# Three moves in a hand-written instruction order: copies of x ahead of squares, x ahead of a product, a crossbar transfer ahead of a load

## The chip, the cores and the metric

The kernel runs on one core of a Trainium2 chip. The core has five engines that run their own instruction streams: TensorE (PE in the profile, with its weight loads listed apart as PEld), VectorE (DVE), ScalarE (ACT), GpSimd (POOL) and SyncE (SP), and 16 DMA engines beside them. The metric is device time in microseconds (us). The kernel before the change takes 170.55 us, the median of three runs (170.48 to 170.65).

## The reference

The first part is a linear-attention recurrence over four batches, eight heads, 768 steps and 48 columns a head; the second is a two-layer network with a squared relu on its result:

```python
def _attn_ref(r, k, v, w, u):
    ...
    for t in range(S):
        kt, vt, rt = (k[:, :, t].copy(), v[:, :, t].copy(), r[:, :, t].copy())
        cur = np.einsum('bhd,bhe->bhde', u[None] * kt, vt)
        y[:, :, t] = np.einsum('bhd,bhde->bhe', rt, state + cur)
        state = w[None, :, :, None] * state + np.einsum('bhd,bhe->bhde', kt, vt)
    return y.astype(np.float32)

def _moe_ref(x, w_in, w_out):
    h = np.maximum(x @ w_in, 0.0)
    return (h * h @ w_out).astype(np.float32)
```

`x` is the result of the first part with the heads side by side: 3072 tokens of 384 values. `w_in` is 384 by 2048, `w_out` is 2048 by 384. Inputs and result are float32; the kernel multiplies in bfloat16.

## The kernel before

**Units and groups.** The 3072 tokens are cut into 24 units of 128 steps, each one chunk of one batch (`UNITS`). The recurrence is done chunk by chunk: inside a unit with matrices, between the units of a batch through a state S. Units are gathered in 14 groups for the network: 0, 1, 12 and 13 hold one unit each, the others two (group 2 is units 2 and 3, group 4 is units 6 and 7, group 8 is units 14 and 15).

**Steps.** Each piece of work is a step, named in a table, with its engine behind the colon (P, D, A, G, S for PE, DVE, ACT, POOL, SP) and the numbers of the buffers that it takes behind the slash. For a unit i the steps are, in order:

- `ld.r`, `ld.k`, `ld.v`: loads on SP's queue (line 322);
- `kh`, `rh`: k and r times powers of w, to bf16 (338, 341); `vb`: v to bf16;
- `P0`: r times k (344); `P1`: that times u (348); `du`: its sum over a head (351); `dv`: v times that sum (356);
- `T` and `Tc`: eight transposes of kh and rh on PE and one copy of them out of PSUM; later units use `XB` in their place, a transposing DMA (405);
- `A`: k against r (412); `Bm`: the masked copy of it (420); `Y`: the unit's output in PSUM (460, 462);
- `xs`: Y plus dv, to bf16 (493; for units 0 to 3 a plain copy); `U`, `ts`, `S`: the state's update (482, 499, 502);
- `X`: three transposes of xs on PE (507), and `xTc`: the copy of them to the network's input (line 252 on ACT, 254 on DVE); for units 12, 15 and 16 to 23 `xX` in their place, a transposing DMA (514) on SP's queue.

For a group g and a slice s of the hidden layer, `F1.g.s` multiplies x by a part of `w_in` into a PSUM bank (523), `re` is the relu out of the bank (533 on ACT, 535 on DVE), `sq` the square (540, 542). `F2.i.q` multiplies a quarter of the squares of unit i by `w_out` (551); four of them fill a bank that `os` copies and `out` writes to memory.

**What sets the order.** Nothing is scheduled: the string `ORDER` is read step by step, and each engine gets its steps in that order and runs them in that order. The loop behind it is

```python
    for step in ORDER.split():
        what, how = step.split(":")
        ...
        getattr(Do, name)(E[eng], *at)
```

The waits are put in when the program is built: an instruction waits for the last writer and the last readers of what it touches, through one counter for each engine. DMAs of SP and ACT use eight counters in turn, and each DMA also waits until the transfer that used its counter before it has landed, so that a place in SP's queue also decides which earlier transfer is waited for. Eight PSUM banks serve everything that PE writes; the bank numbers are those in the table. A step that wants a bank waits until the step that read the bank last is done: `F1.4.7`, for example, takes the bank that `ts.7` reads, `F1.4.5` the one that `ts.8` reads, and `F1.2.1` the one that `Tc.4` reads.

Of the kernel before, what the change touches and what calls it, by code (L numbers as in the profile page):

```python
# [31 lines left out]
Bp.1.0.1:D/4 UP.1:P/4/6 Bp.1.0.0:D/6 X.0:P/5 xs.1:A/1 xTc.0:D/0 S0.2:D Ap.1.1:P/2/0 X.1:P/3 F1.0.3:P/7 ts.3:D/0  # L32
xTc.1:A/1 F1.1.3:P/5 P0.3:G/3 P1.3:G du.2:D/2 re.0.3:D/0 F1.0.0:P/6 Bp.1.1.1:D/5 dv.2:G Wt.2:A re.0.0:A/1 W.1:G
du.3:D/3 ld.v.5:S/5 Wk.2:A F1.1.0:P/4 F1.1.1:P/3 dv.3:G re.1.0:A/2 F1.0.1:P/0 rh.5:G/4 re.1.3:A/3 Bp.1.1.0:D/7
YD.1:P/1/7 YI.3:P sq.1.3:A/0 re.0.1:A/4 W.2:G xs.3:D/2 xs.2:A/3 kh.4:D/5 re.1.1:A/5 sq.1.0:D/1 ld.k.6:S/6 W.3:G
F1.0.2:P/6 X.2:P/4 rh.4:D/5 sq.0.0:A/2 X.3:P/2 F1.1.2:P/5 W.0:G re.0.2:D/3 xTc.3:A/0 sq.0.3:A/3 xTc.2:D/0 re.1.2:A/2
P0.4:D/4 T.4:P/0 Tc.4:D/4 F1.2.4:P/1 F1.2.7:P/4 sq.1.2:D/4 F1.2.5:P/5 re.2.4:D/1 re.2.7:A/0 ld.r.6:S/6 sq.0.2:A/5
F1.2.1:P/0 re.2.5:D/2 re.2.1:A/3 sq.2.5:D/6 sq.0.1:D/7 F1.2.0:P/6 kh.5:D/4 F1.2.2:P/4 sq.2.1:A/8 F1.2.6:P/5 re.2.2:A/2
re.2.0:D/4 T.5:P/0 re.2.6:D/3 F2.0.2:P/4 F1.2.3:P/6 ld.r.7:S/7 Tc.5:A/5 P1.4:D du.4:D/4 sq.1.1:D/9 A.4:P/5/0 A.5:P/1/2
sq.2.6:A/10 re.2.3:A/5 sq.2.3:A/11 F2.0.1:P/4 sq.2.0:A/12 F2.0.3:P/4 vb.4:G/4 Bm.4.1:D/0 Bm.4.0:D/1 sq.2.7:A/13  # L40
# [615 lines left out]
```

## Time and profile before

| | us |
|---|---|
| median of three runs | 170.55 (170.48 to 170.65) |
| the profiled execution | 170.8 |
| its span, first to last instruction | 169.1 |
| PE matmuls busy | 161.0 |
| DVE busy | 137.4 |
| POOL busy | 101.3 |
| ACT busy | 100.6 |

The span is the part of an execution that the trace shows; 1.7 us of this one lie around it. The granted TensorE clock was 1.0 throughout. Matmuls are pipelined, so the busy time of PE counts the overlap of each with the next; where PE waits is read from the distance between starts. In rows of a timeline the first number is the start in us from the span's start, the second the length in us from the first start to the last end of the row's `xN` instructions, and a bracket gives the idle time of the engine before them with what the profile takes for its end.

### The profile page before, as it was taken

The numbers are of one execution on the slowest core, as the hardware profiler recorded it, in microseconds if no ns is written. First come the engines' busy times: TensorE is split into PE (matmuls) and PEld (weight loads), VectorE is DVE, ScalarE is ACT, GpSimd is POOL, SyncE is SP. The second block draws the span as 40 slices with busy tenths as digits, with TensorE's granted clock in tenths as the row PEclk, the third lists the DMA queues.
The fourth block names the chain that finished last, engine by engine and source line by source line (L and its number), as shares of the span: only waits on it lengthen the run. The fifth ranks groups of instructions, "written<-read, shape, count | busy, mean of one in ns | idle before, by whom it ended". The sixth has DMA issues, their size and how long they took to land.

```text
span 169.1 us, 4580 instructions
## 1 busy us (share of the span) xinstructions
PE 161.0 (95%) x1814; PEld 122.5 (72%) x1814; DVE 137.4 (81%) x253; ACT 100.6 (60%) x189; POOL 101.3 (60%) x125
## 2 busy tenths in 40 slices
PE   4998989999997999999999999999999999999993
PEld 1686878668765776888766878766888676898762
DVE  5699769987899999989998998998779975955400
ACT  4696596851771878349782467952099393254731
POOL 6799861295399318996699988399627760300000
DMA  5999999994999899899986999995939751330032
GB/s 135 323 237 192 217 212 203 180 211 88 194 211 170 177 190 222 194 199 188 227 123 134 223 174 214 219 186 144 179 70 202 204 134 25 103 88 0 6 140 93
DMA packets 97785, 28.02 MB, mean 166 GB/s; under 512 B 92530, under 2 KB 97524, under 8 KB 97764
## 3 DMA queue, kind: packets, MB, share of 16 engines
q1 hardware_dynamic: 93872, 22.42, 67.7%
q0 software_dynamic: 3008, 4.13, 12.4%
q10 hardware_dynamic: 884, 1.18, 2.3%
q8 instruction: 14, 0.23, 0.6%
q14 instruction: 7, 0.06, 0.1%
HBM read 20.45 MB, written 4.72 MB: 149 GB/s over the span
## 4 chain that ended last, share of the span: by engine, by line
PE 82%; DVE 8%; DMA 3%; issue 2%; SPq 2%; ACT 1%; DVEq 0%
PE bank L523 36%; PE bank L551 34%; PE bank L412 3%; DMA ldk<-in_k_dram 3%; PE bank L462 2%; SPq L326 2%; PE bank L460 2%; DVE Bm L393 2%; PE bank L482 2%; PE bank L565 2%; PE bank L507 1%; DVE Bm L420 1%; DVE du L351 1%; DVE P L348 1%; DVE P L344 1%
## 5 line engine op out<-in xcount | busy, mean ns | idle before, releaser
L523 PE MATMUL bank<-xT,W 128*128 128x256 bf16 (+1 forms) x672 | 70.2, 257 | 1.3 <-DVE xT L254 0.6
L551 PE MATMUL bank<-W,hq 128*128 128x384 bf16 x368 | 68.6, 326 | 0.0
L523 PEld LDWEIGHTS <-W 128*128 128x128 bf16 x672 | 56.8, 98 | 9.7 <-DVE xT L254 1.2
L533 ACT ACTIVATE hr<-bank 128x512 bf16<-128x512 f32 x67 | 38.9, 595 | 38.2 <-PE bank L523 29.8
L551 PEld LDWEIGHTS <-hq 128*128 128x128 bf16 x368 | 33.8, 97 | 18.5
L540 ACT ACTIVATE hq<-hr 128x512 bf16<-128x512 bf16 x70 | 41.0, 626 | 4.7 <-DVE hr L535 4.1
L420 DVE TENSOR_TENSOR Bm<-bank,maskJT 128x512 bf16<-128x512 f32 x40 | 25.6, 682 | 2.7 <-PE bank L412 2.7
L535 DVE TENSOR_SCALAR hr<-bank 128x512 bf16<-128x512 f32 x29 | 19.8, 686 | 6.7 <-PE bank L523 4.3
L348 POOL TENSOR_TENSOR P<-P,ub 128x384 f32<-128x384 f32 x15 | 16.0, 1070 | 13.2 <-DVE P L344 12.8
L356 POOL TENSOR_TENSOR dv<-ldv,du 128x384 f32<-128x384 f32 (+1 forms) x18 | 15.5, 872 | 13.4 <-DVE du L351 8.3
L341 POOL TENSOR_TENSOR rk<-ldr,Wt 128x384 bf16<-128x384 f32 x15 | 16.4, 1101 | 0.1
L542 DVE TENSOR_TENSOR hq<-hr 128x512 bf16<-128x512 bf16 x26 | 13.0, 513 | 2.0 <-ACT hr L533 1.8
L344 POOL TENSOR_TENSOR P<-ldr,ldk 128x384 f32<-128x384 f32 x13 | 13.3, 1021 | 1.5 <-DMA ldk<-in_k_dram 1.2
L502 POOL TENSOR_TENSOR S0W<-ts,WLm 128x384 bf16<-128x384 f32 x10 | 10.9, 1091 | 4.2 <-DVE ts L499 3.4
L338 POOL TENSOR_TENSOR rk<-ldk,Wk 128x384 bf16<-128x384 f32 x12 | 12.3, 1033 | 1.4 <-DMA ldk<-in_k_dram 1.4
L351 DVE TENSOR_REDUCE du<-P 128x8 f32<-128x384 f32 x24 | 12.9, 542 | 0.0
L493 DVE TENSOR_TENSOR xs<-bank,dv 128x384 bf16<-128x384 f32 x20 | 11.0, 551 | 2.3 <-POOL dv L356 0.7
L254 DVE COPY os<-bank 128x384 f32<-128x384 f32 x11 | 6.1, 551 | 6.5 <-PE bank L551 6.4
L252 ACT COPY xT<-bank 128x384 bf16<-128x384 bf16 x8 | 3.7, 480 | 10.8 <-PE bank L507 10.8
L499 DVE TENSOR_TENSOR ts<-bank,S0W 128x384 f32<-128x384 f32 x16 | 8.8, 549 | 1.1 <-POOL S0W L502 0.8
L462 PE MATMUL bank<-vb,Bm 128*128 128x48 bf16 x160 | 9.5, 184 | 0.0
L252 ACT COPY os<-bank 128x384 f32<-128x384 f32 (+2 forms) x14 | 6.3, 459 | 4.5 <-PE bank L551 2.5
(81 smaller groups left out, 175.0 us busy)
## 6 DMA issues: line engine op xcount, KB each, us to landing
ldr<-in_r_dram SPq DMA_DIRECT2D x20, 192.0 KB, 3.5
ldk<-in_k_dram SPq DMA_DIRECT2D x20, 192.0 KB, 4.0
ldv<-in_v_dram SPq DMA_DIRECT2D x20, 192.0 KB, 3.6
out_dram<-os SPq DMA_DIRECT2D x9, 192.0 KB, 2.3
W<-in_moe_w_in_dram POOLq DMA_DIRECT2D x4, 384.0 KB, 9.7
W<-in_moe_w_out_dram POOLq DMA_DIRECT2D x4, 384.0 KB, 7.4
out_dram<-os ACTq DMA_DIRECT2D x5, 192.0 KB, 3.9
out_dram<-os POOLq DMA_DIRECT2D x5, 192.0 KB, 3.7
```

The source lines that it names most:

```text
L341: e.tensor_mul(rk[slot[f"rk{i}"]][:, 0, :, 0:D], loaded("r", i), Do.factor("t", i % 2 if i < PAIRED else 2))
L344: e.tensor_mul(P0b[slot[f"P{i}"]], loaded("r", i), loaded("k", i))
L348: e.tensor_mul(t, t, bank("bu")[:, 0 : H * D].rearrange("p (h d) -> p h d", h=H) if i in EARLY_U else ub)
L351: e.tensor_reduce(dub[slot[f"dv{i}"]], P0b[slot[f"P{i}"]], axis=mybir.AxisListType.X, op=ALU.add)
L356: e.tensor_mul(dv_of(i) if i < PAIRED else dvb[slot[f"dv{i}"]], loaded("v", i), t)
L420: e.tensor_mul(Bmb[slot[f"Bm{i}{h}"]], heads(bank(f"bA{i}{h}"), 128), mask_b)
L523: e.matmul(hp[:, fi, :], W1[f // 4][:, c, 256 * (f // 2 % 2) : 256 * (f // 2 % 2 + 1)].rearrange("p (m j) -> p j m", j=2)[:, f % 2, :], xt ...
L533: e.activation(hr, hp, AF.Relu)
L535: e.tensor_scalar_max(hr, hp, 0.0)
L540: e.activation(hq, hr, AF.Square)
L542: e.tensor_mul(hq, hr, hr)
L551: e.matmul(bank(f"bO{i}")[:, 0:d_model], hqb[slot[f"hq{g},{f // m}"]][:, at : at + L], W2[q][:, f % 4, :], start=(seen[i] == 1 and f % 4 = ...
```

## The change

Only the table's order changes; no step, engine, buffer or bank does. Three places are touched.

1. **The copies of x of units 2 and 3** (around 23 to 25 us). `X.3` follows `X.2` as before, and `xTc.3` (ACT) and `xTc.2` (DVE) now come straight behind them. On ACT `xTc.3` goes ahead of the square `sq.0.0`; on DVE `xTc.2` goes ahead of `sq.1.0`, `rh.4` and `re.0.2`. On PE the first product that needs both, `F1.2.4`, goes ahead of the transposes `T.4`.
2. **x of units 6 and 7** (around 53 us). On DVE `xs.6` and `xs.7` go ahead of `P0.8`, the product of r and k of unit 8.
3. **The crossbar transfer of unit 15** (around 96 us). On SP `xX.15` goes ahead of the load `ld.v.16`. With it the two exchange counters: `xX.15` now waits for the landing of `ld.v.14`, and `ld.v.16` for that of `xX.12`; `out.8` still waits for `xX.15`, and `XB.19` for `ld.v.16`.

Of the table's lines one pair shows the form, that of the third place:

```diff
-Bm.14.0:D/4 Y.15:P/5 vb.14:G/7 du.14:D/0 F1.7.3:P/1 ld.v.16:S/1 kh.19:G/0 xs.15:D/4 xX.15:S/0 F1.7.2:P/7 re.7.3:A/0
+Bm.14.0:D/4 Y.15:P/5 vb.14:G/7 du.14:D/0 F1.7.3:P/1 kh.19:G/0 xs.15:D/4 xX.15:S/0 ld.v.16:S/1 F1.7.2:P/7 re.7.3:A/0
```

What it does to the engines' streams follows, with the buffers' numbers in the names. On DVE at the first place, `rk` on line 338 is `kh.4`, `xT2` is `xTc.2`, `hq_1` is `sq.1.0`, `rk` on line 341 is `rh.4`, `hr_3` is `re.0.2`, `P_4` is `P0.4` and `rkT` is `Tc.4`:

```order
 L254 CAST xs_2_122<-bank_7_181 128x384
 L338 TENSOR_TENSOR rk_5_80<-ldk_2_69,Wk_200 128x8x48
+L254 COPY xT2_0_127<-bank_4_178 128x3x128
 L542 TENSOR_TENSOR hq_1_137<-hr_2_132 128x512
 L341 TENSOR_TENSOR rk_5_80<-ldr_2_65,Wt_201 128x8x48
 L535 TENSOR_SCALAR hr_3_133<-bank_6_180 128x512
-L254 COPY xT2_0_127<-bank_4_178 128x3x128
 L344 TENSOR_TENSOR P_4_86<-ldr_2_65,ldk_2_69 128x384
 L254 COPY rkT_4_109<-bank_0_174 128x1024
```

The copy moved up three instructions; `P0.4` and `Tc.4` behind it have the same instructions ahead of them as before. On DVE at the second place, `hr_1` is `re.3.5`, `P_3` is `P1.9`, `P_4` is `P0.8`, `xs_1` and `xs_2` are `xs.6` and `xs.7`, `rk_3` is `kh.11` and `ts_0` is `ts.7`:

```order
 L535 TENSOR_SCALAR hr_1_131<-bank_4_178 128x512
 L348 TENSOR_TENSOR P_3_85<-P_3_85,ub_194 128x384
-L344 TENSOR_TENSOR P_4_86<-ldr_0_63,ldk_0_67 128x384
 L493 TENSOR_TENSOR xs_1_121<-bank_5_179,dv_2_94 128x384
 L493 TENSOR_TENSOR xs_2_122<-bank_4_178,dv_1_93 128x384
+L344 TENSOR_TENSOR P_4_86<-ldr_0_63,ldk_0_67 128x384
 L338 TENSOR_TENSOR rk_3_78<-ldk_1_68,Wk_200 128x8x48
 L499 TENSOR_TENSOR ts_0_172<-bank_5_179,S0W_3_193 128x384
```

`P0.8` moved behind the two sums; `kh.11` and `ts.7` stay behind all three. On SP at the third place, the loads of r are `ld.r.19` and `ld.r.18`, the transfer is `xX.15`, the load of v is `ld.v.16`, and the two writes are `out.9` and `out.6`:

```order
 L322 DMA ldr_1_64<-in_r_dram 128x8x48 x2
 L322 DMA ldr_2_65<-in_r_dram 128x8x48
+L514 DMA_TRANSPOSE xT2_0_127<-xs_4_124 128x3x128
 L322 DMA ldv_0_71<-in_v_dram 128x8x48
-L514 DMA_TRANSPOSE xT2_0_127<-xs_4_124 128x3x128
 L604 DMA out_0_dram<-os_1_165 128x384
 L604 DMA out_0_dram<-os_7_171 128x384
```

The transfer and the load changed places; the queue behind them is the same. POOL's stream does not change.

More of the change, by code (lines that the diff above doesn't have):

```diff
@@ L34 @@
 du.3:D/3 ld.v.5:S/5 Wk.2:A F1.1.0:P/4 F1.1.1:P/3 dv.3:G re.1.0:A/2 F1.0.1:P/0 rh.5:G/4 re.1.3:A/3 Bp.1.1.0:D/7
-YD.1:P/1/7 YI.3:P sq.1.3:A/0 re.0.1:A/4 W.2:G xs.3:D/2 xs.2:A/3 kh.4:D/5 re.1.1:A/5 sq.1.0:D/1 ld.k.6:S/6 W.3:G
-F1.0.2:P/6 X.2:P/4 rh.4:D/5 sq.0.0:A/2 X.3:P/2 F1.1.2:P/5 W.0:G re.0.2:D/3 xTc.3:A/0 sq.0.3:A/3 xTc.2:D/0 re.1.2:A/2
-P0.4:D/4 T.4:P/0 Tc.4:D/4 F1.2.4:P/1 F1.2.7:P/4 sq.1.2:D/4 F1.2.5:P/5 re.2.4:D/1 re.2.7:A/0 ld.r.6:S/6 sq.0.2:A/5
+YD.1:P/1/7 YI.3:P sq.1.3:A/0 re.0.1:A/4 W.2:G xs.3:D/2 xs.2:A/3 kh.4:D/5 re.1.1:A/5 ld.k.6:S/6 W.3:G F1.0.2:P/6
+X.2:P/4 X.3:P/2 xTc.3:A/0 sq.0.0:A/2 xTc.2:D/0 sq.1.0:D/1 rh.4:D/5 F1.1.2:P/5 W.0:G re.0.2:D/3 sq.0.3:A/3 re.1.2:A/2
+P0.4:D/4 F1.2.4:P/1 T.4:P/0 Tc.4:D/4 F1.2.7:P/4 sq.1.2:D/4 F1.2.5:P/5 re.2.4:D/1 re.2.7:A/0 ld.r.6:S/6 sq.0.2:A/5
 F1.2.1:P/0 re.2.5:D/2 re.2.1:A/3 sq.2.5:D/6 sq.0.1:D/7 F1.2.0:P/6 kh.5:D/4 F1.2.2:P/4 sq.2.1:A/8 F1.2.6:P/5 re.2.2:A/2
@@ L49 @@
 rh.8:G/2 F2.4.0:P/0 ld.k.10:S/3 Bm.7.0:D/1 Bm.6.0:D/2 Bm.6.1:D/3 sq.3.7:A/21 rh.9:G/1 S.3:G F2.4.1:P/0 re.3.5:D/1
-ld.v.8:S/0 XB.9:S/0 P1.9:D dv.6:G out.2:S F2.4.3:P/0 rh.11:G/3 F2.5.0:P/6 ld.v.9:S/1 P0.8:D/4 sq.3.4:A/22 Y.6:P/5
-rh.10:G/5 ld.r.13:S/5 sq.3.5:A/23 F2.5.3:P/6 xs.6:D/1 Y.7:P/4 X.6:P/5 kh.8:G/2 F2.5.1:P/6 xs.7:D/2 xTc.6:A/2 kh.11:D/3
+ld.v.8:S/0 XB.9:S/0 P1.9:D dv.6:G out.2:S F2.4.3:P/0 rh.11:G/3 F2.5.0:P/6 ld.v.9:S/1 sq.3.4:A/22 Y.6:P/5 rh.10:G/5
+ld.r.13:S/5 sq.3.5:A/23 F2.5.3:P/6 xs.6:D/1 Y.7:P/4 X.6:P/5 kh.8:G/2 F2.5.1:P/6 xs.7:D/2 P0.8:D/4 xTc.6:A/2 kh.11:D/3
 X.7:P/4 U.7:P/5 kh.10:G/5 F2.4.2:P/0 xTc.7:A/2 ts.7:D/0 XB.11:S/2 vb.8:A/0 F1.4.1:P/4 os.4:A/4 S.7:D F1.4.7:P/5
```

## The prediction

> **What bounds the kernel now.** I read the page first, then PE's waits by stretches of the span, then the timelines of the three places.
>
> ```profile
> PE 161.0 (95%) x1814; PEld 122.5 (72%) x1814; DVE 137.4 (81%) x253; ACT 100.6 (60%) x189; POOL 101.3 (60%) x125
> ...
> 24.00:47.40 23.40, 22.93 (x219) 17.15 (x217) 20.98 (x41) 14.24 (x26) 9.95 (x11) 1.00 0.94 177
> 47.40:57.00 9.60, 8.44 (x97) 6.02 (x96) 9.55 (x14) 4.64 (x10) 8.60 (x10) 1.00 1.13 197
> 57.00:93.00 36.00, 36.00 (x401) 27.45 (x399) 33.88 (x61) 24.43 (x46) 27.05 (x28) 1.00 0.99 182
> 93.00:102.00 9.00, 8.71 (x98) 7.06 (x97) 9.00 (x15) 5.08 (x10) 8.18 (x10) 1.00 1.02 196
> 102.00:126.00 24.00, 24.00 (x255) 18.18 (x254) 20.84 (x39) 13.59 (x27) 16.12 (x19) 1.00 0.88 172
> ```
>
> The columns are the stretch, its length, then the busy time of PE, PEld, DVE, ACT and POOL. PE bounds the kernel: between 24 and 126 us it idles 0.47, 1.16 and 0.29 us, 1.92 in all, and each of the three edits stands at one of these three gaps. So each can be worth its gap at most (a little more where the overlap of matmuls hides idle time), and only if nothing behind it eats the lead. In the second and fourth stretch DVE is busy 9.55 of 9.60 and 9.00 of 9.00: there it decides.
>
> **First place: x of units 2 and 3.**
>
> ```profile
> 22.95 0.51 PE L507 MATMUL bank<-identity,xs 128*128 128x128 bf16 x6
> 23.96 0.73 PE L399 MATMUL bank<-identity,rk 128*128 128x128 bf16 x8
> 25.16 4.76 PE L523 MATMUL bank<-xT,W 128*128 128x256 bf16 x42 [0.47 <-DVE xT L254]
> 29.76 0.61 PE L399 MATMUL bank<-identity,rk 128*128 128x128 bf16 x8
> ...
> 22.89 0.55 DVE L338 TENSOR_TENSOR rk<-ldk,Wk 128x384 bf16<-128x384 f32 x1
> 24.16 0.69 DVE L535 TENSOR_SCALAR hr<-bank 128x512 bf16<-128x512 f32 x1
> 24.76 0.35 DVE L254 COPY xT<-bank 128x384 bf16<-128x384 bf16 x1
> 25.02 0.55 DVE L344 TENSOR_TENSOR P<-ldr,ldk 128x384 f32<-128x384 f32 x1
> 25.49 0.69 DVE L254 COPY rkT<-bank 128x1024 bf16<-128x1024 bf16 x1
> ...
> 26.67 1.37 DVE L535 TENSOR_SCALAR hr<-bank 128x512 bf16<-128x512 f32 x2
> 29.21 1.51 DVE L535 TENSOR_SCALAR hr<-bank 128x512 bf16<-128x512 f32 x2
> ...
> 23.79 0.49 ACT L252 COPY xT<-bank 128x384 bf16<-128x384 bf16 x1
> 32.20 0.60 ACT L533 ACTIVATE hr<-bank 128x512 bf16<-128x512 f32 x1 [0.25 <-DVE hq L542]
> ```
>
> The transposes `X.2` and `X.3` are done at 22.95 + 0.51 = 23.46. `xTc.2` can start behind `kh.4` (22.89 + 0.55 = 23.44, less the 0.08 by which neighbours on DVE overlap) and ends at about 23.71. `xTc.3` starts at 23.50 and ends at 23.99. PE starts 0.05 after a copy's end (24.76 + 0.35 = 25.11, then 25.16), so `F1.2.4` starts at about 24.05, when PE is through with `F1.1.2` (23.96). Six matmuls take 0.66 (42 of them from 25.16 to 29.76, and the next work of PE starts 0.16 before the last one's end at 29.92); `T.4` takes 0.45 (as `T.5`, 0.61 less that overlap), and needs `rh.4`, on DVE by 24.51. The next product, `F1.2.7`, then starts at 25.16 in place of 25.82: PE is 0.66 ahead.
>
> DVE does not follow. `P0.4` stays at 25.02, since the same five instructions stand ahead of it; `Tc.4` stays at 25.49, as `T.4` ends at 25.32. From there DVE works without a pause but for two waits on PE: evictions in a row start 0.60 apart (24.16, 24.76), so two take 1.29; the rows with 1.37 and 1.51 hold 0.08 and 0.22 of waiting, and that is what DVE gains: 0.30. The square behind them (`sq.1.1`) releases ACT's eviction at 32.20, which waited 0.25 for it, and ACT's squares then release PE's `F2.3.2` at 35.08. There PE's lead is cut to DVE's: 0.29. What is late next is DVE; from 36 to 47 us its work waits for PE again and moves along. On ACT `re.1.2` slips by 0.23, since `sq.0.0` now waits for `xTc.3`; `F1.2.5`, which wants its bank, comes at 25.82 and it ends at 25.52. Ends: 0 (all of it eaten) and 0.66 (PE's own lead); I take 0.29, the chain that the rows show.
>
> **Second place: x of units 6 and 7.**
>
> ```profile
> 54.50 0.34 PE L507 MATMUL bank<-identity,xs 128*128 128x128 bf16 x3 [1.16 <-DVE xs L493]
> 56.32 1.47 PE L523 MATMUL bank<-xT,W 128*128 128x256 bf16 x12
> 61.24 0.82 PE L523 MATMUL bank<-xT,W 128*128 128x256 bf16 x6
> ...
> 52.63 1.35 DVE L344 TENSOR_TENSOR P<-ldr,ldk 128x384 f32<-128x384 f32 x1
> 53.90 1.01 DVE L493 TENSOR_TENSOR xs<-bank,dv 128x384 bf16<-128x384 f32 x2
> 54.83 1.38 DVE L338 TENSOR_TENSOR rk<-ldk,Wk 128x384 bf16<-128x384 f32 x1
> 56.13 0.54 DVE L499 TENSOR_TENSOR ts<-bank,S0W 128x384 f32<-128x384 f32 x1
> 60.45 0.55 DVE L499 TENSOR_TENSOR ts<-bank,S0W 128x384 f32<-128x384 f32 x1
> ...
> 51.29 2.27 POOL L341 TENSOR_TENSOR rk<-ldr,Wt 128x384 bf16<-128x384 f32 x2
> 53.52 2.27 POOL L338 TENSOR_TENSOR rk<-ldk,Wk 128x384 bf16<-128x384 f32 x2
> ```
>
> `P0.8` takes 1.35 here against 0.55 for `P0.4` at 25.02, where POOL was idle. It ends 0.42 after POOL's pair of products (51.29 + 2.27 = 53.56, then 53.98); `kh.11` ends 0.42 after the next pair (55.79, then 56.21). So a DVE product with both inputs in SBUF and a POOL product take turns, while the two sums `xs`, which read PSUM, run at 0.55 beside POOL.
>
> In the new order `xs.6` starts at 52.63, `X.6` at 53.23 in place of 54.50; `xs.7` waits for the last product of unit 7, which ends where PE's wait begins (54.50 - 1.16 = 53.34), and ends at 53.94. `P0.8`, at 53.87, finds `kh.8` (from 53.52) at work; `kh.8`, with nothing before it now, ends at 54.52, `P0.8` at 54.94, `kh.10` 0.85 later at 55.79, `kh.11` at 56.21: as before, since the same four take turns. So `ts.7` stays at 56.13 to 56.67, and `F1.4.7`, the second half of the row at 56.32 (56.97), wants its bank: 56.73 at the earliest, 0.24 gained out of 1.27. At 61.24 `F1.4.5` wants the bank of `ts.8`, which DVE ends at 61.00 whatever PE does: 61.06, so 0.18 is left. All of it moves by the first place's 0.29 as well. If POOL kept the turn instead, `P0.8` would wait for `kh.10` too (55.49), end at 55.91, and `kh.11`, alone at 0.55, at 56.38; `ts.7` would end at 56.85 and `F1.4.7` gain 0.07. Ends: 0 (the turn lost, and once more later) and 1.16; I take 0.18, since in both rows the engine that already waited went next.
>
> The Trainium skill has a rule for this (SBUF — State Buffer, Who interferes with whom): a VectorE instruction with two SBUF inputs and a GpSimd instruction that reads SBUF exclude each other, and the one that issues first holds the ports until its end. By that rule `P0.8`, issued at 53.87, goes before `kh.10`, issued at 54.49, and the sum has 0.18; read as an advantage for the engine whose next instruction stands ready, it would have 0.07. The two waits of 0.42 above agree with the first.
>
> **Third place: the transfer of unit 15.**
>
> ```profile
> 95.16 0.55 DVE L493 TENSOR_TENSOR xs<-bank,dv 128x384 bf16<-128x384 f32 x1
> 95.61 0.70 SPq L322 DMA_DIRECT2D ldv<-in_v_dram  x1
> 96.41 1.50 SPq L514 DMA_TRANSPOSE xT<-xs  x1
> ...
> xT<-xs SPq DMA_TRANSPOSE x1, 4.9
> ...
> DMA to landing us min/median/max: 2.4/2.4/2.4
> ...
> DMA  9999999999999999997309900000100000699999
> q8 instruction: 1, 0.02, 1.6%
> ...
> 100.13 0.17 PEld L507 LDWEIGHTS <-xs 128*128 128x128 bf16 x3 [0.30 <-DVE xs L493]
> 100.31 0.82 PE L523 MATMUL bank<-xT,W 128*128 128x256 bf16 x6
> 101.40 1.47 PE L523 MATMUL bank<-xT,W 128*128 128x256 bf16 x12 [0.27 <-ACT hq L540]
> 102.20 0.50 ACT L252 CAST vb<-ldv 128x384 bf16<-128x384 f32 x1
> ```
>
> `xX.15` is issued at 96.41 and lands 4.9 later, at 101.3; the row with 2.4 is `xX.12` at 89.4. The digits are the DMA engines from 96.41 to 101.40: nearly still from 99.4 to 100.6, and the one odd transfer in that time is a block of instructions. I read it so that this block held up the transfer's last packets on one engine. `F1.8.7` starts at 101.40, 0.1 after the landing (the profile's name for that wait, a square on ACT, feeds nothing there); without it, it would start at 100.31 + 0.66 = 100.97.
>
> Moved, `xX.15` waits for `xs.15` (95.71) and is issued at 95.77. It lands between 98.2 (2.4) and 100.7 (4.9): by both ends before 100.97. So the gain is 0.43, whatever the landing time; only the tail's end could take some of it. The load pays: `ld.v.16` goes from 95.61 to about 97.3. Its user is the copy `vb.16` on ACT at 102.20, or 101.3 with all leads; even a landing 4.9 later, 102.2, delays ACT by 0.9, and the next thing that PE wants from there, the bank of `re.8.7`, it wants some 1.8 after it is free: no cost. The rest of SP's queue issues as much as before. From 102 to 126 PE is never idle, and DVE's evictions there wait for PE, so the lead reaches the end.
>
> **The sum.** 0.29 + 0.18 + 0.43 = 0.90 off the profiled execution's 170.8 (169.1 of span, 1.7 around it) gives 169.9. That execution stands 0.25 above the median of the runs, so I forecast 170.55 - 0.90 = 169.65.
>
> **Rivals.** (a) *The leads are eaten.* DVE is busy 33.88 of 36.00 from 57 to 93; if another of its waits lies in the way, the first two leads are lost and 0.43 or less stays: 170.1 to 170.5. Against it: PE has no gap there, and the waits that I followed (`ts.8`, `xs.8`, the masked copies) start from PE. (b) *More.* The weight loads of `X.14` idle 0.30 for `xs.14`, which DVE does late because two of its products ahead of it wait their turn behind POOL; with DVE 0.47 earlier it may win those turns. PE could use 0.17 of that (`F1.7.7` at 99.30 + 0.66 = 99.96, against 100.13): 0.90 + 0.17, or 169.48. (c) *Slower.* The block of instructions comes with PE's progress, the transfers with SP's queue. If the new spacing puts it on another transfer that PE needs soon, that one lands up to 2.5 late (4.9 against 2.4). `xX.18` is nearest: PE needs it at 126.58, 0.23 after its landing. It decides from 1.0 of delay; with 1.3 to 2.4 the time is 170.9 to 171.9. Against it: both move together if PE sets both. (d) *The moves do nothing*, as each gap is refilled by the next late step: 170.55; the turns on POOL in the second place come close to that.
>
> **How the numbers follow.** The forecast's case 0.52, (b) 0.16, (a) 0.13, (d) 0.07, (c) 0.12. A measurement of this kernel tells 0.2% (0.34 us) from no change: (a) counts half as same. Faster 0.75, same 0.12, slower 0.13. The range 169.2 to 170.55 leaves out (c) and the far side of (b).
>
> **What would show it.** In the changed trace: PE's product at 25.16 starts near 24.1 and `F2.3.2` about 0.3 earlier; `X.6` starts 1.2 or more earlier, but `ts.7` no more than 0.3; `xX.15` lands before PE has done `F1.7.0`, and the wait of 0.27 is gone; all behind 102 stands 0.9 earlier. Wrong would make it: a later `ts.7`, a new wait on DVE between 57 and 93, or a transfer that lands late behind 102.

## The result and the profile after

The changed kernel takes 169.81 us (median of 15 runs, 169.39 to 170.22) beside 171.03 for the kernel before, measured with it: a ratio of 0.9931 (0.9913 to 0.9949), or 1.18 us less (0.87 to 1.49). The forecast gain was 0.90, near the low end of that; the forecast time of 169.65 was reckoned from the 170.55 of the first runs, and the kernel before came out half a microsecond longer in the later ones. The profiled execution of the changed kernel took 169.43, with a span of 167.7, against 170.8 and 169.1 before. It is the second fastest of the fifteen, so the steps read from it below add up to more (1.36) than the runs gain by the ratio (1.18).

The page and the windows of the changed kernel (PE, PEld, DVE, ACT, POOL; then clock, DMA share, GB/s):

```profile
PE 161.4 (96%) x1814; PEld 123.4 (74%) x1814; DVE 136.3 (81%) x253; ACT 100.9 (60%) x189; POOL 101.4 (60%) x125
...
24.00:47.40 23.40, 23.34 (x223) 17.45 (x220) 21.16 (x43) 14.55 (x26) 10.66 (x12) 1.00 0.99 184
47.40:57.00 9.60, 8.73 (x101) 6.35 (x100) 9.36 (x15) 5.16 (x10) 7.94 (x9) 1.00 1.10 193
57.00:93.00 36.00, 36.00 (x399) 27.29 (x397) 33.88 (x61) 23.84 (x45) 27.92 (x29) 1.00 1.00 188
93.00:102.00 9.00, 9.00 (x108) 7.97 (x106) 8.51 (x15) 5.83 (x12) 8.54 (x10) 1.00 0.94 201
102.00:126.00 24.00, 24.00 (x253) 18.16 (x251) 21.42 (x39) 14.21 (x28) 16.35 (x19) 1.00 0.90 172
```

The idle time of PE from 24 to 126 us fell from 1.92 to 0.93: 0.06 is left at the first place, 0.87 at the second, none at the third. The same places in the timeline of the changed kernel, PE's rows of each first:

```profile
25.13 1.25 PE L523 MATMUL bank<-xT,W 128*128 128x256 bf16 x10
...
34.59 1.47 PE L551 MATMUL bank<-W,hq 128*128 128x384 bf16 x8
...
23.40 0.36 DVE L254 COPY xT<-bank 128x384 bf16<-128x384 bf16 x1
...
26.14 0.42 DVE L542 TENSOR_TENSOR hq<-hr 128x512 bf16<-128x512 bf16 x1
...
26.11 0.81 POOL L254 CAST vb<-ldv 128x384 bf16<-128x384 f32 x1 [2.30 <-DMA ldv<-in_v_dram]
...
52.74 0.34 PE L507 MATMUL bank<-identity,xs 128*128 128x128 bf16 x3
...
54.55 0.82 PE L523 MATMUL bank<-xT,W 128*128 128x256 bf16 x6
56.24 0.81 PE L523 MATMUL bank<-xT,W 128*128 128x256 bf16 x6 [0.87 <-DVE ts L499]
...
53.35 1.08 DVE L344 TENSOR_TENSOR P<-ldr,ldk 128x384 f32<-128x384 f32 x1
54.36 1.36 DVE L338 TENSOR_TENSOR rk<-ldk,Wk 128x384 bf16<-128x384 f32 x1
55.64 0.55 DVE L499 TENSOR_TENSOR ts<-bank,S0W 128x384 f32<-128x384 f32 x1
...
53.03 2.27 POOL L338 TENSOR_TENSOR rk<-ldk,Wk 128x384 bf16<-128x384 f32 x2
...
99.21 0.33 PE L507 MATMUL bank<-identity,xs 128*128 128x128 bf16 x3
99.38 2.13 PE L523 MATMUL bank<-xT,W 128*128 128x256 bf16 x18
...
95.94 0.42 DVE L542 TENSOR_TENSOR hq<-hr 128x512 bf16<-128x512 bf16 x1
...
96.07 1.15 POOL L344 TENSOR_TENSOR P<-ldr,ldk 128x384 f32<-128x384 f32 x1 [0.42 <-DMA ldr<-in_r_dram]
...
95.04 1.47 SPq L514 DMA_TRANSPOSE xT<-xs  x1
```

Read from the starts, PE's lead grows in four steps: 0.49 at `F2.3.2` (34.59 against 35.08), 0.73 at `F1.4.7` (56.24 against 56.97), 0.92 at `X.14` (99.21 against 100.13) and 1.36 at `F1.8.7` (100.04, the second group in the row of 18, against 101.40). It stays 1.36 to the last matmul. So the profiled gain is 0.49 + 0.24 + 0.19 + 0.44 where the sum had 0.29 + 0.18 + 0 + 0.43.

Two of these steps rest on a square on DVE beside an operation on POOL. In the kernel before both squares were the ones that waited:

```profile
26.09 0.65 DVE L542 TENSOR_TENSOR hq<-hr 128x512 bf16<-128x512 bf16 x1
...
25.97 0.50 POOL L254 CAST vb<-ldv 128x384 bf16<-128x384 f32 x1 [2.28 <-DMA ldv<-in_v_dram]
...
96.69 1.18 DVE L542 TENSOR_TENSOR hq<-hr 128x512 bf16<-128x512 bf16 x1
...
96.59 1.00 POOL L344 TENSOR_TENSOR P<-ldr,ldk 128x384 f32<-128x384 f32 x1 [0.21 <-DMA ldr<-in_r_dram]
```

`sq.1.2` stood behind the copy `vb.4` and took 0.65, `sq.7.3` behind the product `P0.21` and took 1.18. In the changed kernel both take 0.42, and it is the POOL operation that is longer. Both POOL operations start when a load has landed (the brackets), not when DVE is ready, so their turn against DVE is open.

### The profile page after: what moved, and what is told of

The parts are those of the page before. It is cut to its first block, busy times and chain, and to the rows that moved or that the text cites. A ratio compares the mean times of both kernels' runs of the same rounds, so it can differ in the third digit from the quotient of the medians.

```text
span 167.7 us, 4580 instructions
## 1 busy us (share of the span) xinstructions
PE 161.4 (96%) x1814; PEld 123.4 (74%) x1814; DVE 136.3 (81%) x253; ACT 100.9 (60%) x189; POOL 101.4 (60%) x125
## 3 DMA queue, kind: packets, MB, share of 16 engines
q10 hardware_dynamic: 884, 1.18, 2.3%
## 4 chain that ended last, share of the span: by engine, by line
PE 87%; DVE 5%; ACT 4%; issue 2%; ACTq 0%
PE bank L523 34%; PE bank L551 34%; PE bank L412 3%; PE bank L365 2%; PE bank L462 2%; PE bank L460 2%; ACT hq L540 2%; PE bank L565 2%; PE bank L482 2%; PE bank L507 1%; DVE hr L535 1%; PE bank L385 1%; PE bank L270 1%; PE bank L304 1%; PE bank L273 1%
## 5 line engine op out<-in xcount | busy, mean ns | idle before, releaser
L254 POOL CAST vb<-ldv 128x384 bf16<-128x384 f32 x10 | 6.7, 673 | 4.0 <-DMA ldv<-in_v_dram 4.0
```

## The experiments

The table gives, for each kernel, the start of five PE steps against the kernel before in the profiled execution (us, negative is earlier), how `xX.15` fared, and the ratio of times. "Block" is the 16 KB of PE instructions (queue q8) that the trace shows near 98 us. The row after_again is the changed kernel in a second execution. In the diffs a line of the order table is cut down to the steps around the change, and `...` stands between two places.

| | `F2.3.2` | `F1.4.7` | `X.14` | `F1.8.7` | end | `xX.15` issued, landed | block | ratio |
|---|---|---|---|---|---|---|---|---|
| before | 0 | 0 | 0 | 0 | 0 | 96.41, 101.26 | 98.65-99.93 | 1 |
| changed kernel | -0.49 | -0.73 | -0.92 | -1.36 | -1.36 | 95.04, 98.16 | 97.59-98.80 | 0.9931 (0.9913-0.9949) |
| after_again | -0.19 | -0.43 | -0.47 | -0.90 | -0.61 | 95.30, 98.26 | 97.68-98.84 | none |
| e1_copies | -0.28 | -0.28 | -0.46 | -0.47 | -0.47 | 96.36, 100.79 | 98.40-99.45 | 0.9969 (0.9955-0.9983) |
| e1_copies_only | -0.33 | -0.33 | -0.52 | -0.12 | -0.12 | 96.38, 101.15 | 98.66-100.07 | 0.9988 (0.9973-1.0002) |
| e1_cast_later | -0.49 | -0.51 | -0.61 | -0.79 | -0.64 | 96.00, 100.47 | 98.25-99.44 | 0.9964 (0.9952-0.9977) |
| e2_sums | 0.01 | -0.23 | -0.22 | -0.09 | -0.08 | 96.33, 101.18 | 98.87-99.81 | 0.9984 (0.9969-1.0000) |
| v1_ts7_first | -0.28 | -1.56 | -1.58 | -2.02 | -1.91 | 94.42, 97.62 | 96.93-97.98 | 0.9908 (0.9891-0.9925) |
| e3_transfer | 0.22 | 0.22 | 0.23 | -0.20 | -0.20 | 95.95, 99.07 | 98.61-99.56 | 0.9981 (0.9969-0.9994) |
| e12_both_moves | -0.42 | -0.67 | -0.86 | -0.87 | -0.64 | 96.12, 100.39 | 97.86-99.02 | 0.9958 (0.9942-0.9974) |
| e13_without_sums | -0.51 | -0.50 | -0.69 | -0.90 | -0.90 | 95.40, 100.36 | 98.33-99.26 | 0.9943 (0.9928-0.9958) |
| p1_block_shift | 0.06 | 0.05 | -0.13 | -0.57 | 0.17 | 97.86, 100.61 | 96.22-97.22 | 0.9997 (0.9982-1.0013) |
| e3_square_first | 0.00 | -0.02 | -0.20 | -0.64 | -0.64 | 95.72, 98.75 | 98.33-100.23 | 0.9957 (0.9945-0.9970) |
| v2_both_more | -0.22 | -1.51 | -1.53 | -1.80 | -1.80 | 94.90, 99.46 | 97.46-98.39 | 0.9898 (0.9876-0.9919) |

A trace is one execution; the ratios come from several. The columns are therefore read for mechanisms and the ratios for what a kernel is worth.

### The first place

**e1_copies**: the first edit alone. Two of its three pairs of lines are shown; in the pair ahead of them `sq.1.0` goes out of the line and `F1.0.2` comes in.

```diff
-F1.0.2:P/6 X.2:P/4 rh.4:D/5 sq.0.0:A/2 X.3:P/2 F1.1.2:P/5 W.0:G re.0.2:D/3 xTc.3:A/0 sq.0.3:A/3 xTc.2:D/0 re.1.2:A/2
-P0.4:D/4 T.4:P/0 Tc.4:D/4 F1.2.4:P/1 F1.2.7:P/4
+X.2:P/4 X.3:P/2 xTc.3:A/0 sq.0.0:A/2 xTc.2:D/0 sq.1.0:D/1 rh.4:D/5 F1.1.2:P/5 W.0:G re.0.2:D/3 sq.0.3:A/3 re.1.2:A/2
+P0.4:D/4 F1.2.4:P/1 T.4:P/0 Tc.4:D/4 F1.2.7:P/4
```

> The first edit alone. Theory of DVE's chain: F1.2.4 starts 1.1 earlier and T.4 0.7 later, PE is 0.66 to 0.70 ahead up to F2.1.1, and at F2.3.2 (35.08 before) the lead is cut to what DVE gained: 0.49 if the square sq.1.2 (0.65 before) runs in 0.42 ahead of POOL's copy vb.4, 0.29 if it waits behind that copy as before. The second gap (1.16) stays whole, and so does the wait for xX.15 behind it, because the instruction block that holds the transfer up comes with PE's progress: the end moves by as much as F2.3.2, 170.1 to 170.3 beside 170.55 for before. Rival, the lead is eaten: F2.3.2 under 0.1 earlier and no change of the time.

The time fell to 170.37, 0.53 less by the ratio. The timeline of this kernel has `sq.1.2` behind `vb.4`, and the lead at `F2.3.2` is 0.28:

```profile
26.14 0.64 DVE L542 TENSOR_TENSOR hq<-hr 128x512 bf16<-128x512 bf16 x1
...
26.00 0.50 POOL L254 CAST vb<-ldv 128x384 bf16<-128x384 f32 x1 [2.19 <-DMA ldv<-in_v_dram]
...
34.80 1.47 PE L551 MATMUL bank<-W,hq 128*128 128x384 bf16 x8
...
99.84 0.82 PE L523 MATMUL bank<-xT,W 128*128 128x256 bf16 x6
100.93 0.82 PE L523 MATMUL bank<-xT,W 128*128 128x256 bf16 x6 [0.27 <-DMA xT<-xs]
```

The second gap is whole (1.2 us), and the wait for `xX.15` is still there, as expected (0.42 by the starts). What was missed is `X.14`: it gains 0.18 more, since DVE's lead of 0.28 brings `sq.7.3` ahead of `P0.21` (0.42 long here), by no margin: the two start at the same moment, 96.40.

**e1_cast_later**: the first edit, and POOL's `vb.4` behind `dv.4`.

```diff
-F2.0.3:P/4 vb.4:G/4 Bm.4.1:D/0
+F2.0.3:P/4 Bm.4.1:D/0
...
-dv.4:G Y.4:P/0
+dv.4:G vb.4:G/4 Y.4:P/0
```

> The first edit, with POOL's copy vb.4 behind dv.4, so that nothing of POOL's stands beside the square sq.1.2. Theory that this square's turn against vb.4 is worth the 0.2 between the first edit's runs: sq.1.2 takes 0.42 however early ld.v.4 lands, and F2.3.2 is 0.49 earlier than before (0.28 in the run of the first edit alone, 0.49 in the changed kernel): 170.05. Rival, the difference has another cause: F2.3.2 stays 0.28 earlier, 170.3. A loss would show as Y.4 (34.16 in the changed kernel) waiting for the later vb.4, whose end is expected near 32.9.

```profile
26.14 0.41 DVE L542 TENSOR_TENSOR hq<-hr 128x512 bf16<-128x512 bf16 x1
...
32.26 0.49 POOL L254 CAST vb<-ldv 128x384 bf16<-128x384 f32 x1
...
34.16 0.36 PE L462 MATMUL bank<-vb,Bm 128*128 128x48 bf16 x8
34.58 1.47 PE L551 MATMUL bank<-W,hq 128*128 128x384 bf16 x8
```

With POOL out of the way the square takes 0.41 and `F2.3.2` comes 0.49 earlier, as in the changed kernel's own trace; `Y.4` at 34.16 pays nothing. So the 0.2 between the runs of the first edit is this one turn. At the end it is 0.64: `F1.8.7` still waits 0.25 for `xX.15`, and `F1.10.5` loses 0.15 to a late `xX.18`. The ratio of 0.9964 can't be told from that of e1_copies, so how much this turn is worth in time, over many executions, is left open.

**e1_copies_only**: the first edit without its part on PE.

```diff
-P0.4:D/4 F1.2.4:P/1 T.4:P/0 Tc.4:D/4
+P0.4:D/4 T.4:P/0 F1.2.4:P/1 Tc.4:D/4
```

> The first edit without its part on PE: the copies of x are early, but T.4 stays ahead of F1.2.4. T.4 wants rh.4, which now stands behind xTc.2 and ends at 24.56, so PE waits for it in place of the copy: T.4 ends near 24.95, F1.2.4 starts at 24.9 in place of 25.17, a lead of 0.27. Theory of DVE's chain: F2.3.2 was held to 0.28 to 0.49 by DVE in the full edit, so up to 0.27 of this arrives and the edit on PE is worth 0.0 to 0.2 at the end. Rival: without the swap nothing is gained, because Tc.4 comes no earlier.

`T.4` waits 0.26 for `rh.4`, `F1.2.4` starts at 24.85 (24.90 was expected), and the lead of 0.33 arrives whole at `F2.3.2`. With `sq.1.2` at 0.41 in both, e1_cast_later has 0.49 there: the swap on PE is worth 0.16. In this run `xX.15` landed 0.36 later than in e1_copies and took most of the lead back (the end is 0.12 earlier), so the ratio says little of the first place.

### The second place

**e2_sums**: the second edit alone.

```diff
-F2.5.0:P/6 ld.v.9:S/1 P0.8:D/4 sq.3.4:A/22 Y.6:P/5
+F2.5.0:P/6 ld.v.9:S/1 sq.3.4:A/22 Y.6:P/5
...
-F2.5.1:P/6 xs.7:D/2 xTc.6:A/2
+F2.5.1:P/6 xs.7:D/2 P0.8:D/4 xTc.6:A/2
```

> The second edit alone. Theory of turns at the shared port: X.6 starts 1.27 earlier, but P0.8, kh.8, kh.10 and kh.11 take turns to the same end, ts.7 ends at 56.7 as before, F1.4.7 is 0.24 earlier and no more; the end 0.2 to 0.3 earlier, 170.3. Rival, POOL keeps the turn: P0.8 ends behind kh.10, ts.7 ends 0.18 later, F1.4.7 gains 0.07. Rival, the whole gap is worth its 1.16: F1.4.7 over 0.8 earlier.

`X.6` starts 1.27 earlier, `F1.4.7` 0.23, and PE waits 0.9 for `ts.7` in between. `P0.8` ends at 54.94, `kh.8` at 54.53, `kh.10` at 55.80, `kh.11` at 56.22 (forecast: 54.94, 54.52, 55.79, 56.21). The step is worth 0.24 to 0.25 in each trace that has it without more: here, in e12_both_moves, and twice in the changed kernel. In time it is 0.27 by the ratio, at the edge of what can be told from nothing; in the trace 0.15 of the 0.23 was lost at `F1.8.7`, where `xX.15` had landed only 0.08 earlier, and 0.08 is left at the end.

**v1_ts7_first**: the changed kernel with `ts.7` ahead of `kh.11` on DVE.

```diff
-P0.8:D/4 xTc.6:A/2 kh.11:D/3
+P0.8:D/4 xTc.6:A/2
...
-xTc.7:A/2 ts.7:D/0 XB.11:S/2
+xTc.7:A/2 ts.7:D/0 kh.11:D/3 XB.11:S/2
```

> The changed kernel, with the state's sum ts.7 ahead of kh.11 on DVE. Theory of turns at the port: kh.11 waits for POOL's kh.10 until 55.3 in any order, so ts.7, which reads PSUM, fits into that wait: it ends near 54.9, F1.4.7 follows F1.4.1 without a gap at 55.21 (56.24 in the changed kernel), kh.11 still ends near 55.7. Behind it DVE's ts.8 is 0.5 earlier, which lets F1.4.5 keep 0.6 to 0.75: the end about 0.6 below the changed kernel's, 169.2. Rival, ts.7 is not what F1.4.7 waits for, or another step of DVE takes the lead back by 62: under 0.2 gained.

```profile
54.57 0.54 DVE L499 TENSOR_TENSOR ts<-bank,S0W 128x384 f32<-128x384 f32 x1
55.04 0.89 DVE L338 TENSOR_TENSOR rk<-ldk,Wk 128x384 bf16<-128x384 f32 x1
...
53.24 2.27 POOL L338 TENSOR_TENSOR rk<-ldk,Wk 128x384 bf16<-128x384 f32 x2
...
54.76 1.47 PE L523 MATMUL bank<-xT,W 128*128 128x256 bf16 x12
```

`F1.4.1` and `F1.4.7` are one row of twelve matmuls now, with no wait between, and `kh.11` ends 0.42 after POOL's pair (55.93 after 55.51) although it starts later. That is the state's sum running in the time that `kh.11` had spent waiting. From `F2.3.2` on the second place is worth 1.28 here against 0.24 in the changed kernel; `F1.4.5`, which waits for `ts.8`, keeps 1.11 of it. The time is 169.16, a ratio of 0.9908 to the kernel before; the changed kernel's 0.9931 has an interval that overlaps with it, so that v1 is the faster of the two rests on the trace.

The Trainium skill (SBUF — State Buffer, Who interferes with whom) says that a VectorE instruction with at most one SBUF input, outside the modes that take both of VectorE's port pairs, does not contend with GpSimd. This trace agrees: `ts.7` and both `xs` sums, with one input in PSUM, take 0.54 to 0.56 beside POOL's products.

### The third place

**e3_transfer**: the third edit alone.

```diff
-F1.7.3:P/1 ld.v.16:S/1 kh.19:G/0 xs.15:D/4 xX.15:S/0 F1.7.2:P/7
+F1.7.3:P/1 kh.19:G/0 xs.15:D/4 xX.15:S/0 ld.v.16:S/1 F1.7.2:P/7
```

> The third edit alone. Up to 96 us nothing changes. xX.15 is issued 0.64 earlier and lands by 100.7, so F1.8.7 starts when PE is through with F1.7.0: 100.97 in place of 101.40 where DVE still does sq.7.3 behind POOL's P0.21 (sq.7.3 takes about 1.2, X.14 waits for xs.14): 0.43 off, 170.1. Rival: the gain at X.14 comes from the third edit too, then sq.7.3 takes 0.42 here and F1.8.7 starts near 100.8. Rival, the landing is not what F1.8.7 waits for: no gain.

From `F2.3.2` on, 0.42 is gained at `F1.8.7`, which follows `F1.7.0` with no wait; `sq.7.3` takes 1.21 behind `P0.21`, and `X.14` gains nothing. The 0.22 that is lost at the first place has no edit behind it: `ld.v.4` landed at 30.43 in this execution (25.91 in the one of before), and `vb.4` then came beside `P1.4`, which took 0.75 in place of 0.55. The ratio, 0.32 less, holds the 0.43 within its interval (0.10 to 0.53).

**e12_both_moves**: the first two edits, without the third (the two diffs above).

> The first two edits without the third. If the three gains are separate: F1.4.7 0.73 earlier as in the full change, and from there on PE 0.73 earlier. With DVE that much earlier, sq.7.3 goes ahead of P0.21 (0.42 in place of 1.18) and X.14 does not wait: 0.92 earlier there, as in the full change. Theory of the instruction block: it moves with PE, falls on xX.15 again, and the wait at F1.8.7 is back, 0.4 to 0.5 long, so the end is 0.7 to 0.8 earlier: 169.8. Rival, the late landing is a thing of where the transfer stands against other transfers or chance: with the new spacing xX.15 lands within 3.2 of its issue and the end is 1.2 to 1.36 earlier without the third edit.

```profile
99.44 0.82 PE L523 MATMUL bank<-xT,W 128*128 128x256 bf16 x6
100.53 1.14 PE L523 MATMUL bank<-xT,W 128*128 128x256 bf16 x9 [0.27 <-DMA xT<-xs]
```

The wait for `xX.15` is back, 0.43 by the starts. The block had moved with PE (97.86) and the transfer with SP, and they met again. `X.14` gained its 0.19 (0.86), but not as expected: `sq.7.3` went behind `P0.21` and took 1.00. Of this lead 0.23 was lost at `F1.10.5`, for which the transfer `xX.18` landed late (125.81): that is the prediction's case (c) at the very place it named, without the third edit.

**e13_without_sums**: the first and third edits, without the second.

> The changed kernel without the second edit. If the second edit is worth the 0.24 that F1.4.7 gained in all three runs that have it, and nothing else hangs on it: F2.3.2 0.28 to 0.49 earlier, the 1.16 gap whole, xX.15 landed long before it is wanted, and sq.7.3 ahead of P0.21 by the first edit's lead alone, as in that edit's own run. F1.8.7 0.28 + 0.60 to 0.49 + 0.60 earlier, the time 0.9 to 1.1 below before, a ratio of 0.9945. Rival: sq.7.3 needs the second edit's lead too and goes behind P0.21; then 0.17 less.

`sq.7.3` goes first (96.18, 0.42 long) and `X.14` gains 0.19, by the first edit's lead alone. But `xX.15`, issued at 95.40, landed only 4.96 later, and `F1.8.7` waited 0.23 for it. So the third edit shortens the issue, and does not rule out the late landing. The ratio is 0.9943, 0.97 less, as expected.

**p1_block_shift**: the kernel before, with 52 matmuls of one column at the head of PE's stream. They compute nothing that is used.

```diff
-Z.8:P/0 bw:P/1
+Z.152:P/0 Z.8:P/0 bw:P/1
...
+            if n > 99:
+                for m in range(n - 100):
+                    e.matmul(bank("bZ")[0:1, 0:1], one16[:, 0:1], one16[:, 0:1], start=True, stop=True, skip_group_check=True)
+                return
```

> The kernel before, with 52 one-column matmuls of a constant put at the head of PE's stream, where PE has nothing to do until 4.97 (they write a bank that the first step overwrites). They add 104 instructions, so each block of PE's instructions is fetched 104 instructions earlier: by the kernel before's own order of starts the block at 98.65 comes near 94.8 and is in by 96.1, ahead of the issue of xX.15 at 96.41. Theory of the instruction block: xX.15 now lands 2.4 to 3.2 after its issue in place of 4.85, F1.8.7 starts near 100.97 in place of 101.40, and the kernel is about 0.4 faster without any of the three edits. Rival, the transfer is late because it stands behind the load ld.v.16 in the queue: it lands 4.2 to 4.9 after its issue as before, and nothing is gained.

Nothing was gained (0.9997), and yet the third gap is gone. The timeline of this kernel (its lines stand two lower up to 580, and more behind):

```profile
97.87 1.39 SPq L516 DMA_TRANSPOSE xT<-xs  x1
...
100.17 2.02 PE L525 MATMUL bank<-xT,W 128*128 128x256 bf16 x17
...
120.19 0.83 PE L525 MATMUL bank<-xT,W 128*128 128x256 bf16 x6 [0.57 <-DMA xT<-xs]
```

and its DMA views, the first from 97.87 to 100.62, the second from 116.9 to 120.2:

```profile
xT<-xs SPq DMA_TRANSPOSE x1, 2.7
...
q8 instruction: 1, 0.02, 2.3%
...
xT<-xs SPq DMA_TRANSPOSE x1, 4.4
```

The block came at 96.22 to 97.22 (94.8 to 96.1 was expected), and `xX.15` landed 2.7 after its issue in place of 4.9, although the load `ld.v.16` still stood ahead of it; `F1.8.7` follows without a wait, 0.57 earlier than before. Of this 0.44 is the transfer's; the rest was gained at `X.14`, because `P0.21` started only at 96.95 here and `sq.7.3` (96.74, 0.41 long) went ahead of it, with none of the edits. But the next block came at 117.76 to 118.95, in the middle of `xX.17`, which then took 4.4 and landed at 120.15 (118.74 before), and `F1.9.2` waited 0.57 for it. One weakness: the issue of `ld.v.16` took 1.90 here, so `xX.15` was issued 1.45 later than before, when the block was already in. That the block is the cause rests on this run and on the next two paragraphs together.

**What the traces say together.** In eight of the traces `xX.15` landed 4.3 to 5.0 after its issue, and in all eight the landing was 1.04 to 1.37 after the end of the block (before 1.33, e1_copies 1.34, e2_sums 1.37, e12_both_moves 1.37, e1_cast_later 1.04, e1_copies_only 1.08, e13_without_sums 1.10, v2_both_more 1.07), though the issues are spread over 1.5 us and the blocks over 1.4. In the other six it landed 2.7 to 3.2 after its issue, before the block was through or, in p1_block_shift, behind it. With the third edit the transfer was not held in five of seven traces; without it, in none but the one with the shifted block. In p1_block_shift the same shows at two other places: `xX.17` landed 1.20 after its block, and `XB.6`, wanted by `A.6`, 1.09 after a block at 46.89 to 47.87, so that `A.6` began 0.80 later than before (the second gap swallowed that).

**What was held.** The trace lists each packet, and sixteen landing counts for each transfer. `xX.15` is 384 packets of 256 bytes. In four of the eight held traces (before, e1_copies, e2_sums, e12_both_moves) 360 packets had started well before the block was through; the last 24, one sixteenth, started within 0.02 of its end and took 0.66, and all sixteen counts came 0.5 to 0.7 behind them. In the kernel before they are the 4 to 12 GB/s in the last slices of this row, from 98.0 to 100.6 in slices of 0.065 us:

```profile
GB/s 236 269 251 261 250 277 259 266 270 224 434 158 107 36 0 24 236 307 165 47 0 0 0 0 0 0 0 0 0 8 4 12 8 8 8 12 8 12 8 8
```

That is 6 KB of 96, as much as one DMA engine of sixteen would carry, and it starts as the block ends (99.91 and 99.93): the block held up one engine's part, as the prediction had read it. In the other four (e1_copies_only, e1_cast_later, e13_without_sums, v2_both_more) all 384 packets had started before the block's end and fifteen counts came 2.8 to 3.3 after the issue; one came 1.5 to 1.9 later, 1.04 to 1.10 behind the block. So with the third edit only the one count was ever caught, in two traces of seven. Why it was caught in v2_both_more and e13_without_sums, where the last packet started 0.02 and 0.37 ahead of the block, and not in e3_transfer and e3_square_first (0.08 and 0.11), stays open, and so does the microsecond from the block's end to that count.

**e3_square_first**: the third edit, with `sq.7.3` ahead of `os.8` on DVE.

```diff
-os.8:D/3 re.7.2:A/1 ld.r.20:S/4 sq.7.3:D/17
+sq.7.3:D/17 os.8:D/3 re.7.2:A/1 ld.r.20:S/4
```

> The third edit, with the square sq.7.3 ahead of the copy os.8 on DVE, so that it is issued near 96.35 as soon as re.7.3 is done (96.28), and POOL's P0.21 (from 96.59) comes behind it without any lead from the first two edits. Theory that X.14's wait of 0.17 is that lost turn: sq.7.3 takes 0.42 in place of 1.18, xs.14 ends near 99.0 in place of 100.08, X.14 starts with PE at 99.96, and F1.8.7 is 0.60 earlier than before (0.42 in the third edit's own run, taken from F2.3.2 on): 170.2 by the runs of the third edit at 170.44. Rival: xs.14 is held by dv.14 in any case, then X.14 stays and F1.8.7 gains 0.42.

```profile
96.29 0.42 DVE L542 TENSOR_TENSOR hq<-hr 128x512 bf16<-128x512 bf16 x1
...
96.59 1.00 POOL L344 TENSOR_TENSOR P<-ldr,ldk 128x384 f32<-128x384 f32 x1 [0.78 <-DMA ldr<-in_r_dram]
...
99.94 0.33 PE L507 MATMUL bank<-identity,xs 128*128 128x128 bf16 x3
100.10 1.58 PE L523 MATMUL bank<-xT,W 128*128 128x256 bf16 x13
```

Without any lead from the first two edits `X.14` starts at 99.94 (99.96 expected) and `F1.8.7` 0.64 earlier. So the 0.19 at `X.14` was the lost turn of one square. The ratio, 0.9957 or 0.73 less, is larger than this trace's 0.64, and the runs spread over 170.03 to 170.15 only.

### The two further moves together, and the changed kernel once more

**v2_both_more**: the moves of v1_ts7_first and e1_cast_later on the changed kernel.

> The changed kernel with both further moves: ts.7 ahead of kh.11, and POOL's vb.4 behind dv.4. If the two are separate, F2.3.2 is 0.49 earlier than in the kernel before whatever ld.v.4 does (0.28 in the run of v1_ts7_first), F1.4.7 starts near 55.2 and the time is 0.0 to 0.2 below the 169.16 of v1_ts7_first: 169.0. Rival: the 0.2 is lost again at F1.10.5, which in that run waited for the transfer xX.18; then 169.15.

168.97, a ratio of 0.9898; beside v1_ts7_first (0.9908) that is no difference the intervals allow to tell. The trace doesn't show the expected 0.49 at `F2.3.2`, though `sq.1.2` took 0.42: `F1.0.0` ended 0.28 later than before, at 19.58, for a reason that lies ahead of all the edits, and that is missing from the lead behind it (0.43 at `F1.2.7` in place of 0.70). `xX.15` was held in this run, and cost 0.17. The loss at `F1.10.5` did not come.

**after_again**: the changed kernel unchanged.

> The changed kernel once more, for a second trace. With the third edit xX.15 stood ahead of the instruction block's hold in four runs (landed 3.0 to 3.2 after its issue) and was held by it in two (4.6 and 5.0). If that is settled by the order of instructions, it lands near 98.2 again and F1.8.7 follows F1.7.0 without a gap. If it is settled anew in each execution, it may land near 100.0 here, 4.5 to 5.0 after its issue, and F1.8.7 waits up to 0.2. The first place, by the same view: F2.3.2 0.28 or 0.49 earlier than before, as vb.4 starts before or after sq.1.2 is issued; F1.4.7 0.24 earlier beyond that in either case.

```profile
29.39 0.62 PE L399 MATMUL bank<-identity,rk 128*128 128x128 bf16 x8 [0.17 <-DVE rk L338]
...
27.80 1.07 DVE L542 TENSOR_TENSOR hq<-hr 128x512 bf16<-128x512 bf16 x2
...
27.75 0.50 POOL L254 CAST vb<-ldv 128x384 bf16<-128x384 f32 x1 [3.95 <-DMA ldv<-in_v_dram]
```

170.19, beside 171.06 for the kernel before. `ld.v.4` landed at 27.70 and `vb.4` came beside the next two squares, a third outcome for the first place (0.19). The second place gave 0.24, as always. `sq.7.3` lost its turn again (1.16; `P0.21` was 0.12 ahead), `xX.15` landed 2.96 after its issue, and `xX.18` cost 0.29 at `F1.10.5`. The end is 0.61 earlier than before, against 1.36 in the first trace: the same program, with the same steps won by order and different ones by chance. Both executions lie inside the changed kernel's range of 169.39 to 170.22.

## Why the prediction was right, and where its sum fell short

**The first term, 0.29, took the outcome of one turn as fixed.** The copies ended as reckoned (`xTc.3` at 23.98, forecast 23.99; `F1.2.4` at 24.03, forecast 24.05), and PE's lead was 0.70 (0.66). That DVE cuts it at `F2.3.2` is right; what failed is the sentence that DVE works there "without a pause but for two waits on PE". A third wait was hidden in the length of `sq.1.2`: 0.65, where the same square takes 0.42 alone. Where `vb.4` went first as in the kernel before (e1_copies, v1_ts7_first, 0.64), the lead was 0.28, the forecast's own size; in the profiled run, where the square went first, it was 0.49. In six traces with the whole first edit the square's length and the lead add up to 0.91 to 0.93. The other three are after_again (0.19, a later square lost its turn), v2_both_more (0.22, PE was late ahead of the edit) and e1_copies_only, which leaves out the swap on PE (0.33).

**The second term, 0.18, was right in each step.** Moved by the lead of 0.49, `P0.8`, `kh.10`, `kh.11` and `ts.7` ended within 0.02 of the forecast, and `F1.4.7` gained the 0.24. Of this 0.18 was to be left at `F1.4.5`; in the changed kernel and in e2_sums all of it is left, because `P0.10` (0.86 before) runs in 0.55 ahead of POOL's `vb.9`, which waits for a load. The rival in which POOL keeps the turn did not occur.

**The third term, 0.43, was right in the trace (0.44) and too sure.** "Whatever the landing time" holds while PE is no further ahead: e13_without_sums waited 0.23 for a landing 4.96 after the issue. What it said of the block, that it held up the last packets on one engine, is what the packets show.

**Case (b) came about in the profiled run, and was given 0.16.** `sq.7.3` went ahead of `P0.21` in six of the nine traces that have the first edit or its copies; in the other three (after_again, e12_both_moves, e1_cast_later) and with the second or third edit alone it went behind, and in p1_block_shift it went ahead with none of them. In e12_both_moves `X.14` gained its 0.19 all the same, because the load of `P0.21` had landed 0.87 earlier and the product was through the sooner. That the turn could be won was seen; that in the changed kernel DVE came 0.74 earlier there and `P0.21`, which is tied to a load, only 0.53, is what decided it; since `P0.21` started anywhere from 96.37 to 96.95 in the five traces without the first edit, that is in part luck.

**Case (a)** did not occur: in no trace is the lead at `X.14` more than 0.01 smaller than at `F1.4.5`. **Case (c)** did, in the sister kernels and in the second trace of the changed one, at `F1.10.5` as named; its price was 0.11 to 0.29, and not the 1.25 to 2.25 that its times (170.9 to 171.9, against the 169.65 of the forecast) imply. They don't follow from the prediction's own figures either: a delay of 1.3 to 2.4 that decides from 1.0 costs 0.3 to 1.4. The size was taken from the wrong quantity: `xX.18` lands 1.78 to 2.22 after the block near 122 has ended, in every trace but the shifted one, before included, so it looks held in all of them, and with PE ahead what it loses goes by the length of the block: blocks of 1.24 to 1.45 cost 0.11 to 0.29, blocks of 0.87 to 1.22 nothing. The larger price, 0.73, was paid once, at `F1.9.2` in p1_block_shift.

Within their intervals the three edits add up: the single ratios give 0.9969 x 0.9984 x 0.9981 = 0.9934, against 0.9931 for all. In the single traces they don't (0.47, 0.08 and 0.20 at the end, against 1.36 and 0.61 for all), because each trace won or lost other turns.

That 169.81 lies so near the forecast 169.65 is partly luck: the gain was 0.28 larger than the sum, and the kernel before, from which the time was reckoned, came out 0.48 longer.

## What to carry to other kernels

When a kernel's order is written by hand, an engine that shares a port with another decides its turn by whichever instruction is issued first, and a partner that starts on a load's landing makes that turn a matter of the execution: put an instruction that doesn't need the port (here a sum out of PSUM) where the other would wait, or move the partner out of reach, and the gain no longer hangs on a load: it was there in both traces of each such move (1.28 and 1.29 for `ts.7`, a square of 0.41 and 0.42 for `vb.4`). Before summing the gain of a lead, look through the chain that it runs along for instructions that are longer than their like; each is a wait that no column shows. A transfer with less margin than a block of instructions takes can be late in some executions. The held landings of `xX.15` came at most 2.2 later after their issue than the quickest free one (4.96 against 2.74), so by estimate that much margin would cover them; no run here tried it.

## What the runs showed of the hardware

A block of PE's instructions, 16 KB on one DMA queue, is fetched about every 250 instructions and takes 0.9 to 1.9 us. In the thirteen traces in which one came while `xX.15` was under way, the transfer landed 4.3 to 5.0 after its issue in eight and 3.0 to 3.2 in five. 104 instructions at the head of the stream moved the block from 98.65 to 96.22 and another onto `xX.17`, so a change of a few per cent in the length of PE's program can cost or save half a microsecond elsewhere.

The Trainium skill (DMA: Bandwidth & Descriptors, Queues, rings and completion order) says that each DMA engine takes the descriptors of a ring in order and goes round between the queues that have work for it, packet by packet. That a block on another queue holds up one sixteenth of a transfer's packets until it is through (24 of 384, from 99.91, the block's end being 99.93) agrees with this in kind; that a landing count alone comes 1.04 to 1.10 after the block's end is not explained by it.

The recorded start decides a turn at the port only to about 0.03: `sq.1.2` at 26.141 went ahead of `vb.4` at 26.114, and `sq.7.3` at 96.405 ahead of `P0.21` at 96.404 (e1_copies). Where the starts of these two pairs were 0.07 or more apart, the earlier one went first.
